# Row-tiled leftovers of the down projection in one block, on an S5 + SwiGLU layer

## The chip, the cores and the metric

One core of a Trainium2 chip. The metric is the device time of one execution in microseconds; each kernel is run several times and the median is shown. The profile is of one execution, of which it has every instruction of the engines: TensorE (PE; its weight loads apart as PEld), VectorE (DVE), ScalarE (ACT), GpSimd (POOL) and the queue of SyncE (SP), which here issues nearly all DMAs.

## The reference

A layer norm, and beside each other a diagonal state space model and a SwiGLU feed-forward, added to the input. 2048 tokens, width 512, 512 complex states, hidden width F = 1376.

```python
xn = layernorm(x)                                   # over 512, no weights
# A: state space model
Lam_bar = exp(exp(log_dt) * Lam)
Bu = xn @ B_bar.T                                   # complex, B_bar = ((Lam_bar - 1) / Lam) * B
h[t] = Lam_bar * h[t-1] + Bu[t]                     # 2048 steps
yA = 2 * real(h @ C.T) + xn * Dskip
# B: feed-forward
yB = (silu(xn @ w_gate) * (xn @ w_up)) @ w_down
out = x + yA + yB
```

1376 is 10 x 128 + 96: ten whole tiles of the hidden width, and 96 rows left over. These leftovers are what the change is about.

## The kernel before

The tokens go through in four chunks of 512 (`CH`), each of four tiles of 128. For each chunk:

- layer norm of four tiles into `xn_sb` (`ln_chunk`; statistics on DVE, rstd on POOL; chunks 2 and 3 are normalised on ACT, `ln_apply_act`, L503), then one DMA transpose into `xnT` (`xt_chunk_dma`; chunk 2's transpose lands in a part of the scratch tile `scrC`);
- gate and up matmuls with the hidden width on the partitions (`ffn_gate`, `ffn_up`, L716), 2 x 4 matmuls of 512 columns into a pair of PSUM banks; ACT makes `sg` = silu of the one (L728) and copies the other to `uf` (L785), DVE multiplies them into `hT` (L787);
- B matmuls (L836), copied by ACT to `u_sb` (L843); on DVE a rotation (L867), the scan (L876) and the rotation back into `hss`;
- down and C matmuls (`dc_chunk`), which sum into one bank for each tile of 128 tokens: a "down pass" of ten matmuls with `hT` for each of the four tiles (L919), and then, tile after tile, one leftover matmul of 96 rows (L933, `hL` by the last 96 rows of `w_down`) and eight C matmuls (L936); DVE adds the bank to `x_sb` (L941), in which input and skip stand by then (`resid_chunk`), and SP stores the tile.

The gate and up leftovers of all four chunks are done in one go after chunk 1's matmuls (`ffn_left`, L798 and L808; L808 uses half the columns of the array for each of two chunks), and DVE leaves their products in `hL`, 96 rows for each chunk.

In the last chunk the last tile is done in two pieces, 416 and 96 columns, so that the final addition and store are small.

Order of the work. Every instruction group is a task of a graph (`g.add`, `dma`) with its reads and writes. TensorE and SP keep the order of the program text; for ACT, DVE and POOL a list scheduler (`_schedule`) picks the next task by estimated times and the longest path behind it. `od` holds order edges that carry no data. `_plan` then works out which semaphores a task has to wait for, and `_emit` writes one `wait_ge` after the other ahead of the instruction. The eight PSUM banks are handed out in pairs by `next_pair`. The text order of the last part is: gate and up of chunk 3, `resid_chunk(2)`, `resid_chunk(3)`, `dc_chunk(2)`, `dc_chunk(3, split_last=True)`.

Of the kernel before, what the change touches and what calls it, by code (L numbers as in the profile page):

```python
# [10 lines left out]
ALU = alu_op_type.AluOpType  # L11
F32 = mybir.dt.float32
B16 = mybir.dt.bfloat16
# [171 lines left out]
def _plan(tasks, streams, new_sem, eng_sems):  # L185
    consumers = defaultdict(list)
    for t in tasks:
        for d in t.deps:
            consumers[d].append(t)
    for t in tasks:  # L190
        if t.dma:
            t.nsig = True
        else:
            t.nsig = any((c.eng != t.eng) or (t.eng != "pe") or c.dma for c in consumers[t])
    for eng, st in streams.items():
        lvl = 0
        for t in st:
            if t.dma:
                t.sem = new_sem("dma%d" % t.idx)
                t.lvl = 16  # L200
            elif t.nsig:
                lvl += 1
                t.sem = eng_sems[eng]
                t.lvl = lvl
    pos = {e: 0 for e in streams}
    known = {e: {} for e in streams}
    done = set()
    remaining = sum(len(s) for s in streams.values())
    while remaining:
        progressed = False  # L210
        for eng, st in streams.items():
            while pos[eng] < len(st):
                t = st[pos[eng]]
                if any(d not in done for d in t.deps):
                    break
                kn = known[eng]
                waits = {}
                for d in t.deps:
                    if d.eng == eng and eng == "pe" and not d.dma and not t.dma:
                        continue  # L220
                    k = id(d.sem)
                    if kn.get(k, 0) >= d.lvl:
                        continue
                    if k not in waits or waits[k][1] < d.lvl:
                        waits[k] = (d.sem, d.lvl)
                for d in t.deps:
                    for k, v in d.vc.items():
                        if kn.get(k, 0) < v:
                            kn[k] = v
                t.waits = list(waits.values())  # L230
                t.vc = dict(kn)
                if t.sem is not None:
                    t.vc[id(t.sem)] = max(t.vc.get(id(t.sem), 0), t.lvl)
                done.add(t)
                pos[eng] += 1
                remaining -= 1
                progressed = True
        assert progressed, "deadlock in static schedule"
# [11 lines left out]
def bass_parallel_sum__ssm_conv_s5__swiglu_ffn__prompt_kernel(  # L250
# [17 lines left out]
    Fh = B_w_gate.shape[1]  # L268
# [6 lines left out]
    PT = P // 128  # L275
    FT = (Fh + 127) // 128
    fsz = [min(128, Fh - i * 128) for i in range(FT)]
# [3 lines left out]
    g = _Graph()  # L281
    es = ExitStack()
    with es:
# [33 lines left out]
        tt1 = scrC[:, 1024:2048].rearrange("p (b t) -> p b t", b=2)  # L317
        tz = scrC[:, 2048:3072].rearrange("p (b t) -> p b t", b=2)
        xnT2 = scrC[:, 2048:3072].bitcast(B16).rearrange("p (j k t) -> p j k t", j=4, k=KT)
        xnT = [xnT01[:, 0], xnT01[:, 1], xnT2, xnT3]  # L320
        wtmp = scrC[:, 0:2048].rearrange("p (k d) -> p k d", k=4)
        NUS = 8
# [47 lines left out]
        def next_pair():  # L370
            for _ in range(NB // 2):
                b = 2 * (pair_ctr[0] % (NB // 2))
                pair_ctr[0] += 1
                if not (b in reserved or _bank_live(b) or _bank_live(b + 1)):
                    return b
            raise AssertionError("all PSUM pairs live")
# [4 lines left out]
        def BK(b):  # L381
            return [("bk", b, 0), ("bk", b, 1)]
# [407 lines left out]
        def ffn_left():  # L790
# [22 lines left out]
            for c, bk in zip((0, 2), pairs):  # L813
                sl = gctr[0] % NG
                gctr[0] += 1
                ul = uctr_f[0] % NUF
                uctr_f[0] += 1
                g.add("act", lambda e, sl=sl, bk=bk: e.activation(out=sg[0:NG0, sl].rearrange("p a t -> p (a t)"), in_=pair_f32(slice(0, NG0), bk), func=AF.Silu),
                      reads=BK(bk) + BK(bk + 1), writes=[("sg", sl)], name="silul%d" % c, est=917)
                g.add("act", lambda e, ul=ul, bk=bk: e.activation(out=uf[NU0:NG0, ul].rearrange("p a t -> p (a t)"), in_=pair_f32(slice(NG0, 128), bk), func=AF.Identity),  # L820
                      reads=BK(bk) + BK(bk + 1), writes=[("uf", ul)], name="uevx%d" % c, est=917)
                for k in range(2):
                    g.add("act", lambda e, k=k, ul=ul, c=c: e.activation(out=uf[0:NU0, ul, k, :], in_=pbank[64 * k:64 * k + NU0, bu + c // 2, :], func=AF.Identity),  # L823
                          reads=BK(bu + c // 2), writes=[("uf", ul)], name="uevl%d_%d" % (c, k), est=490)
                g.add("dve", lambda e, sl=sl, ul=ul, c=c: e.tensor_tensor(out=hL[0:NG0, c:c + 2, :], in0=sg[0:NG0, sl], in1=uf[0:NG0, ul], op=ALU.mult),
                      reads=[("sg", sl), ("uf", ul)], writes=[("hL", c + k) for k in range(2)], name="hmull%d" % c, est=611)

        usctr = [0]
        uctr = [0]
# [69 lines left out]
                    g.add("dve", lambda e, t1_=t1_, t3_=t3_, q_=q_: e.tensor_tensor(out=car[:, c + 1, 0, q_], in0=t3_, in1=t1_, op=ALU.subtract), reads=[("sm", "ct3", ph), ("sm", "ct1", ph)], writes=[("car", c + 1, ph)], name="c5_%d_%d" % (c, ph), est=70)  # L899
                    g.add("dve", lambda e, t2_=t2_, t4_=t4_, q_=q_: e.tensor_tensor(out=car[:, c + 1, 1, q_], in0=t4_, in1=t2_, op=ALU.add), reads=[("sm", "ct4", ph), ("sm", "ct2", ph)], writes=[("car", c + 1, ph)], name="c6_%d_%d" % (c, ph), est=70)  # L900

        def dc_chunk(c, split_last=False):
            hb = c % 2
            n = FT + 2 * PT
            items = []
            for lt in range(4):
                if split_last and lt == 3:
                    items.append((lt, 0, 416))
                    items.append((lt, 416, 96))
                else:  # L910
                    items.append((lt, 0, 512))
            prs = [next_pair() for _ in range((len(items) + 1) // 2)]
            banks = [prs[k // 2] + k % 2 for k in range(len(items))]

            def add_A(lt, c0, nc_, bk):
                def mmA(e, bk=bk, lt=lt, hb=hb, c=c, c0=c0, nc_=nc_):
                    for i in range(FL):
                        fs = fsz[i]
                        inst = e.matmul(pbank[:, bk, 0:nc_], lhsT=hT[0:fs, hb, i, lt * 128:(lt + 1) * 128], rhs=wd[0:fs, i, c0:c0 + nc_], start=(i == 0), stop=False)  # L919
                    return inst  # L920
                g.add("pe", mmA, reads=[("hT", hb, i) for i in range(FL)] + [("wd", 0)],
                      writes=BK(bk), name="mm_dA%d_%d" % (4 * c + lt, c0), est=FL * (216 if nc_ == 512 else nc_ * 0.43), ninst=FL)
            for it, bk in zip(items, banks):
                if it[2] >= 256:
                    add_A(*it, bk)
            for (lt, c0, nc_), bk in zip(items, banks):
                a = 4 * c + lt
                if nc_ < 256:
                    add_A(lt, c0, nc_, bk)

                def mmB(e, bk=bk, lt=lt, hb=hb, c=c, c0=c0, nc_=nc_):
                    j = FT
                    e.matmul(pbank[:, bk, 0:nc_], lhsT=hL[0:NG0, c, lt * 128:(lt + 1) * 128], rhs=wd[0:NG0, FL, c0:c0 + nc_], start=False, stop=False)  # L933
                    for pt in range(PT):
                        for ri in range(2):
                            inst = e.matmul(pbank[:, bk, 0:nc_], lhsT=hss[:, hb, pt, ri, lt * 128:(lt + 1) * 128], rhs=W12[:, ri, pt, c0:c0 + nc_], start=False, stop=(j == n - 1))  # L936
                            j += 1
                    return inst
                g.add("pe", mmB, reads=[("hL", c), ("wd", 1)] + [("hss", hb, pt) for pt in range(PT)] + [("W", ri, pt) for ri in range(2) for pt in range(PT)],
                      writes=BK(bk), name="mm_dB%d_%d" % (a, c0), est=(2 * PT + 1) * (216 if nc_ == 512 else nc_ * 0.43), ninst=2 * PT + 1)  # L940
                g.add("dve", lambda e, bk=bk, a=a, c0=c0, nc_=nc_: e.tensor_tensor(out=x_sb[:, a, c0:c0 + nc_], in0=pbank[:, bk, 0:nc_], in1=x_sb[:, a, c0:c0 + nc_], op=ALU.add),  # L941
                      reads=BK(bk) + [("x", a)], writes=[("xo", a, c0)], name="oadd%d_%d" % (a, c0), est=(660 if nc_ == 512 else 100 + nc_))
                dma("st_out%d_%d" % (a, c0), out_v[:, a, c0:c0 + nc_], x_sb[:, a, c0:c0 + nc_], writes=[("out", a, c0)], nbytes=TILEB * nc_ // 512,
                    reads=[("xo", a, c0)], out_=True)

        ffn_gate_quarters([0, 1, 2, 3])
        params_a()
# [40 lines left out]
            ffn_up(3, ip)  # L988
        resid_chunk(2)
        resid_chunk(3)  # L990
        dc_chunk(2)
        dc_chunk(3, split_last=True)

        _DBG["smi"] = dict(SMI)
        _DBG["sbuf_left"] = nc.sbuf_bytes_remaining
# [42 lines left out]
```

## Time and profile before

| | |
|---|---|
| timed runs, us | 178.19, 178.90, 179.28; median 178.9 |
| the profiled execution | 178.13 us, span of the instructions 176.3 us |
| busy, us | PE 173.0, DVE 161.8, ACT 86.1, PEld 82.4, POOL 11.3 |
| chain that ended last | PE 96% of the span |
| TensorE clock granted | full, throughout |
| matmuls L919 / L936 / L933 | 170 / 136 / 17 |
| DMA | 12.37 MB, 70 GB/s over the span |

Busy times of TensorE overlap from one matmul to the next (a 512-column matmul is shown with 379 ns, but they start 216 ns apart), so starts are compared and not lengths. The chain is followed backwards from the last instruction. Releasers of a wait are inferred. POOL's times are rough.

### The profile page before, as it was taken

Reading aid. Unit: us, or ns where it says so; the run is one execution under the profiler, and the core shown is the slowest. Engines: PE = TensorE matmul, PEld = TensorE weight load, DVE = VectorE, ACT = ScalarE, POOL = GpSimd, SP = SyncE. Lnnn points to the kernel's source line nnn. Section 1 sums busy time; section 2 is a strip of 40 time slices with the busy share of each in tenths; the row PEclk is TensorE's granted clock in tenths of the full one; section 3 lists DMA queues with packets and bytes.
Section 4 is the critical chain, followed back from the end, with each engine's and each line's share of the span. In section 5 each row is a group of like instructions: output and inputs, shape, how many; then the busy total and the mean of one; then the engine's idle time right before and its main releaser. Section 6 shows DMA issues by size and latency. Waiting matters only on the chain.

```text
span 176.3 us, 2356 instructions
## 1 busy us (share of the span) xinstructions
PE 173.0 (98%) x914; PEld 82.4 (47%) x914; DVE 161.8 (92%) x277; ACT 86.1 (49%) x113; POOL 11.3 (6%) x22
## 2 busy tenths in 40 slices
PE   7899999999999999999999999999999999999995
PEld 2794444444444444444444444444444444444443
DVE  2873999999999999999999999999999999999953
ACT  4479989899999579220456564000265620000000
POOL 3040500344000000000000000000000000000000
PEclk9999999999999999999999999999999999999999
DMA  5897565566559000002100000001100000000132
GB/s 173 272 368 187 119 114 179 162 132 131 149 205 123 0 0 0 0 4 86 35 0 0 0 0 4 0 0 59 59 0 4 0 0 0 0 0 4 42 118 78
DMA packets 22967, 12.37 MB, mean 70 GB/s; under 512 B 15309, under 2 KB 22957, under 8 KB 22957
## 3 DMA queue, kind: packets, MB, share of 16 engines
q1 hardware_dynamic: 22652, 11.77, 25.0%
q10 hardware_dynamic: 304, 0.46, 0.8%
q8 instruction: 7, 0.11, 0.3%
q14 instruction: 4, 0.02, 0.0%
HBM read 6.46 MB, written 2.10 MB: 49 GB/s over the span
## 4 chain that ended last, share of the span: by engine, by line
PE 96%; DMA 1%; DVE 1%; ACT 0%; issue 0%
PE pb L716 36%; PE pb L919 20%; PE pb L936 16%; PE pb L836 16%; PE pb L759 4%; PE pb L933 2%; PE pb L798 2%; DMA x_sb<-in_A_x_dram 1%; PE pb L808 1%; PE pb L543 1%; DVE st L512 0%; DVE xn_sb L495 0%; ACT xnT L554 0%; DVE x_sb L941 0%; ACT sd L514 0%
## 5 line engine op out<-in xcount | busy, mean ns | idle before, releaser
L876 DVE TENSOR_TENSOR_SCAN rot<-sm,car,rot 128x512 bf16<-128x512 f32 x32 | 38.7, 1265 | 0.0
L728 ACT ACTIVATE sg<-pb 128x1024 bf16<-128x1024 f32 x20 | 20.1, 1023 | 33.0 <-PE pb L716 31.9
L919 PE MATMUL pb<-wd,hT 128*128 128x512 bf16 (+2 forms) x170 | 35.4, 367 | 0.0
L936 PE MATMUL pb<-W,hss 128*128 128x512 bf16 (+2 forms) x136 | 30.4, 366 | 0.0
L716 PE MATMUL pb<-xnT,wu 128*128 128x512 bf16 x120 | 27.9, 379 | 0.0
L919 PEld LDWEIGHTS pb<-wd,hT 128*128 128x128 bf16 x170 | 16.1, 98 | 18.9 <-ACT uf L823 0.4
L785 ACT ACTIVATE uf<-pb 128x1024 bf16<-128x1024 f32 x20 | 20.5, 1025 | 7.9 <-PE pb L716 7.4
L716 PE MATMUL pb<-xnT,wg 128*128 128x512 bf16 x92 | 21.8, 379 | 0.0
L836 PE MATMUL pb<-xnT,BT 128*128 128x512 bf16 x96 | 21.0, 379 | 0.0
L936 PEld LDWEIGHTS pb<-W,hss 128*128 128x128 bf16 x136 | 12.8, 97 | 14.9
L843 ACT ACTIVATE u_sb<-pb 128x1024 bf16<-128x1024 f32 x16 | 16.1, 1020 | 5.6 <-PE pb L836 5.5
L716 PEld LDWEIGHTS pb<-xnT,wu 128*128 128x128 bf16 x120 | 11.7, 98 | 14.2 <-issue 0.2
L836 PEld LDWEIGHTS pb<-xnT,BT 128*128 128x128 bf16 x96 | 9.4, 98 | 11.3
L941 DVE TENSOR_TENSOR x_sb<-pb,x_sb 128x512 bf16<-128x512 f32 (+2 forms) x17 | 10.9, 655 | 3.8 <-PE pb L936 3.2
L787 DVE TENSOR_TENSOR hT<-sg,uf 128x1024 bf16<-128x1024 bf16 x20 | 13.5, 681 | 0.7 <-ACT uf L785 0.7
L716 PEld LDWEIGHTS pb<-xnT,wg 128*128 128x128 bf16 x92 | 9.0, 98 | 10.6
L479 DVE BATCH_NORM_STATS2 st<-x_sb 128x6 f32<-128x512 bf16 x12 | 7.5, 678 | 3.0 <-DMA x_sb<-in_A_x_dram 3.0
L867 DVE TENSOR_TENSOR rot<-u_sb,cosT 128x2048 bf16<-128x2048 bf16 x8 | 9.7, 1217 | 0.0
L867 DVE TENSOR_TENSOR rot<-rot,sin 128x2048 bf16<-128x2048 bf16 x8 | 9.8, 1219 | 0.0
L867 DVE TENSOR_TENSOR rot<-u_sb,sin 128x2048 bf16<-128x2048 bf16 x8 | 9.7, 1215 | 0.0
L867 DVE TENSOR_TENSOR rot<-rot,cosT 128x2048 bf16<-128x2048 bf16 x8 | 9.7, 1212 | 0.0
L867 DVE TENSOR_TENSOR rot<-rot 128x2048 bf16<-128x2048 bf16 x8 | 9.6, 1216 | 0.0
(87 smaller groups left out, 175.8 us busy)
## 6 DMA issues: line engine op xcount, KB each, us to landing
out_dram<-x_sb SPq DMA_DIRECT2D x15, 128.0 KB, 1.7
x_sb<-in_A_x_dram SPq DMA_DIRECT2D x3, 512.0 KB, 4.4
wd<-in_B_w_down_dram SPq DMA_DIRECT2D x1, 1280.0 KB, 6.3
wu<-in_B_w_up_dram SPq DMA_DIRECT2D x1, 768.0 KB, 4.9
wu<-in_B_w_up_dram SPq DMA_DIRECT2D x1, 608.0 KB, 7.1
x_sb<-in_A_x_dram SPq DMA_DIRECT2D x4, 128.0 KB, 3.5
wg<-in_B_w_gate_dram SPq DMA_DIRECT2D x1, 480.0 KB, 5.9
wg<-in_B_w_gate_dram ACTq DMA_DIRECT2D x1, 448.0 KB, 3.8
```

The costliest lines, as they stand in the source:

```text
L479: return g.add("dve", lambda e, a=a: e.bn_stats(out=st[:, a % 8, :], in_=x_sb[:, a, :]), reads=[("x", a)], writes=[("st", a % 8)], name="b ...
L716: inst = e.matmul(pbank[0:fs, bk, :].rearrange("p (j t) -> p j t", j=4), lhsT=w[:, kt, i * 128:i * 128 + fs], rhs=xnT[c][:, :, kt, :], sta ...
L728: g.add("act", lambda e: e.activation(out=sg[rows, sl, 0:n, :].rearrange("p a t -> p (a t)"), in_=pair_f32(rows, bk, 512 * n), func=AF.Sil ...
L785: g.add("act", lambda e: e.activation(out=uf[rows, ul, 0:n, :].rearrange("p a t -> p (a t)"), in_=pair_f32(rows, bk, 512 * n), func=AF.Ide ...
L787: g.add("dve", lambda e: e.tensor_tensor(out=hT[rows, hb, i0:i0 + n, :], in0=sg[rows, sl, 0:n, :], in1=uf[rows, ul, 0:n, :], op=ALU.mult), ...
L836: inst = e.matmul(pbank[:, bk, :].rearrange("p (j t) -> p j t", j=4), lhsT=BT[:, ri, kt, pt * 128:(pt + 1) * 128], rhs=xnT[c][:, :, kt, :] ...
L843: g.add("act", lambda e: e.activation(out=u_sb[:, us].rearrange("p r t -> p (r t)"), in_=pair_f32(slice(0, 128), b0), func=AF.Identity), r ...
L867: tt = lambda out, a, b, op, r, w, nm: g.add("dve", lambda e: e.tensor_tensor(out=out, in0=a, in1=b, op=op), reads=r, writes=w, name="%s_% ...
L876: g.add("dve", lambda e, A0=A0, A1=A1, k=k, ri=ri, pt=pt: e.tensor_tensor_scan(out=A1[:, k, ri, :], data0=rr[:, pt:pt + 1].to_broadcast([1 ...
L919: inst = e.matmul(pbank[:, bk, 0:nc_], lhsT=hT[0:fs, hb, i, lt * 128:(lt + 1) * 128], rhs=wd[0:fs, i, c0:c0 + nc_], start=(i == 0), stop=F ...
L936: inst = e.matmul(pbank[:, bk, 0:nc_], lhsT=hss[:, hb, pt, ri, lt * 128:(lt + 1) * 128], rhs=W12[:, ri, pt, c0:c0 + nc_], start=False, sto ...
L941: g.add("dve", lambda e, bk=bk, a=a, c0=c0, nc_=nc_: e.tensor_tensor(out=x_sb[:, a, c0:c0 + nc_], in0=pbank[:, bk, 0:nc_], in1=x_sb[:, a, ...
```

## The change

It has three parts.

1. `dc_chunk(2)` and `dc_chunk(3, split_last=True)` become `dc_last(2)`. The down passes of chunks 2 and 3 stand one after the other, in all eight banks. Then one block, `mmL`, does the leftovers of both chunks (all but the last 96 columns): the 96 rows are cut into three slices of 32, and each of the four token tiles `lt` has its operands on the partitions 32 `lt` to 32 `lt` + 31, so that 24 matmuls of 32 rows take the place of eight of 96. Then follow the C passes of both chunks, and the last piece of 96 columns as before. The operands are copies made by twelve new DMAs on SP: `wdL` (the leftover rows of `w_down`, four times) and `hR` (pieces of `hL`, eight), in parts of `scrC` that are free once W is prepared. All matmuls of the block have the tile size 32 x 128.
2. Chunk 2's normalisations on ACT get order edges: tile 9 after the copy of the third B unit of chunk 1, tile 10 after the fourth, tile 11 after the silu of chunk 1's first gate pair. In the program as built, tile 8 comes after the third copy, 9 after the fourth, and 10 and 11 after that silu; the cosine of the last state tile moves from ahead of them to behind them.
3. A task's waits are emitted in the order in which the planner expects them to end (DMAs first), the last one next to the instruction.

```diff
-                for d in t.deps:
+                for d in sorted(t.deps, key=lambda d: (not d.dma, d.fin, d.idx)):
...
                     if k not in waits or waits[k][1] < d.lvl:
+                        waits.pop(k, None)
                         waits[k] = (d.sem, d.lvl)
...
+        NL = 3
+        wdL = scrC[:, 0:768].bitcast(B16).rearrange("p (s d) -> p s d", s=NL)
+        hR = scrC[:, 768:1152].bitcast(B16).rearrange("p (c s t) -> p c s t", c=2, s=NL)
...
+            for r in range(4):
+                dma("ld_wdL%d" % r, wdL[32 * r:32 * r + 32, :, :], B_w_down[FL * 128:Fh, :].rearrange("(i s) d -> i s d", s=NL), [("wdL", r)], NG0 * 1024, after=tuple(alias_H))
+            for c in (2, 3):
+                for r in range(4):
+                    dma("hR%d_%d" % (c, r), hR[32 * r:32 * r + 32, c - 2, :, :], hL[0:NG0, c, r * 128:(r + 1) * 128], [("hR", c, r)], NG0 * 256, reads=[("hL", c)], after=tuple(alias_H))
...
+        def dc_last(c0):
+            items = []
+            for c in (c0, c0 + 1):
+                for lt, bk in enumerate(dc_banks()):
+                    w = 416 if (c, lt) == (c0 + 1, 3) else 512
+                    items.append((c, lt, w, bk))
+                    dc_A(c, lt, 0, w, bk)
+
+            def mmL(e):
+                for h in (items[:4], items[4:]):
+                    for k in range(NL):
+                        for c, lt, w, bk in h:
+                            inst = e.matmul(pbank[:, bk, 0:w], lhsT=hR[32 * lt:32 * lt + 32, c - 2, k, :], rhs=wdL[32 * lt:32 * lt + 32, k, 0:w], start=False, stop=False)
+                return inst
+            g.add("pe", mmL, reads=[("hR", c, r) for c in (2, 3) for r in range(4)] + [("wdL", r) for r in range(4)],
+                  writes=sum([BK(it[3]) for it in items], []), name="mm_dL", est=2 * NL * 216 + 200, ninst=2 * NL * 4)
+            for c, lt, w, bk in items:
+                dc_B(c, lt, 0, w, bk, 0)
+            bk = next_pair()
+            dc_A(c0 + 1, 3, 416, 96, bk)
+            dc_B(c0 + 1, 3, 416, 96, bk, 1)
...
-        dc_chunk(2)
-        dc_chunk(3, split_last=True)
+        dc_last(2)
+
+        by_name = {t.name: t for t in g.tasks}
+        for nm, prev in (("xn9", "uev_b1_2"), ("xn10", "uev_b1_3"), ("xn11", "silu1_0")):
+            by_name[nm].od.add(by_name[prev])
```

`dc_A` is the down pass of one tile, `dc_B` its C pass (with the leftover matmul where its last argument is 1), addition and store; both are the code of `dc_chunk` cut in two. Chunks 0 and 1 keep their leftover matmul of 96 rows.

More of the change, by code (lines that the diff above doesn't have):

```diff
@@ L900, in ssm_elem_chunk, with dc_A @@
                     g.add("dve", lambda e, t2_=t2_, t4_=t4_, q_=q_: e.tensor_tensor(out=car[:, c + 1, 1, q_], in0=t4_, in1=t2_, op=ALU.add), reads=[("sm", "ct4", ph), ("sm", "ct2", ph)], writes=[("car", c + 1, ph)], name="c6_%d_%d" % (c, ph), est=70)
-        def dc_chunk(c, split_last=False):
+        def dc_A(c, lt, c0, nc_, bk):
             hb = c % 2
-            n = FT + 2 * PT
-            items = []
[L906 to L944, printed above, removed]
@@ new lines, in mmA, with dc_B, mmB @@
+            def mmA(e):
+                for i in range(FL):
+                    inst = e.matmul(pbank[:, bk, 0:nc_], lhsT=hT[:, hb, i, lt * 128:(lt + 1) * 128], rhs=wd[:, i, c0:c0 + nc_], start=(i == 0), stop=False)
+                return inst
+            g.add("pe", mmA, reads=[("hT", hb, i) for i in range(FL)] + [("wd", 0)],
+                  writes=BK(bk), name="mm_dA%d_%d" % (4 * c + lt, c0), est=FL * (216 if nc_ == 512 else nc_ * 0.43), ninst=FL)
+        def dc_B(c, lt, c0, nc_, bk, left):
+            hb = c % 2
+            a = 4 * c + lt
+            def mmB(e):
+                if left:
+                    e.matmul(pbank[:, bk, 0:nc_], lhsT=hL[0:NG0, c, lt * 128:(lt + 1) * 128], rhs=wd[0:NG0, FL, c0:c0 + nc_], start=False, stop=False)
+                for pt in range(PT):
+                    for ri in range(2):
+                        inst = e.matmul(pbank[:, bk, 0:nc_], lhsT=hss[:, hb, pt, ri, lt * 128:(lt + 1) * 128], rhs=W12[:, ri, pt, c0:c0 + nc_], start=False, stop=(pt == PT - 1 and ri == 1))
+                return inst
+            g.add("pe", mmB, reads=([("hL", c), ("wd", 1)] if left else []) + [("hss", hb, pt) for pt in range(PT)] + [("W", ri, pt) for ri in range(2) for pt in range(PT)],
+                  writes=BK(bk), name="mm_dB%d_%d" % (a, c0), est=(2 * PT + left) * (216 if nc_ == 512 else nc_ * 0.43), ninst=2 * PT + left)
+            g.add("dve", lambda e: e.tensor_tensor(out=x_sb[:, a, c0:c0 + nc_], in0=pbank[:, bk, 0:nc_], in1=x_sb[:, a, c0:c0 + nc_], op=ALU.add),
+                  reads=BK(bk) + [("x", a)], writes=[("xo", a, c0)], name="oadd%d_%d" % (a, c0), est=(660 if nc_ == 512 else 100 + nc_))
+            dma("st_out%d_%d" % (a, c0), out_v[:, a, c0:c0 + nc_], x_sb[:, a, c0:c0 + nc_], writes=[("out", a, c0)], nbytes=TILEB * nc_ // 512,
+                reads=[("xo", a, c0)], out_=True)
@@ new lines, in dc_banks, with dc_chunk @@
+        def dc_banks():
+            prs = [next_pair() for _ in range(2)]
+            return [prs[lt // 2] + lt % 2 for lt in range(4)]
+        def dc_chunk(c):
+            banks = dc_banks()
+            for lt in range(4):
+                dc_A(c, lt, 0, 512, banks[lt])
+            for lt in range(4):
+                dc_B(c, lt, 0, 512, banks[lt], 1)
+        def dc_last(c0):
+            items = []
+            for c in (c0, c0 + 1):
[8 more added lines that the diff above has]
+                            inst = e.matmul(pbank[:, bk, 0:w], lhsT=hR[32 * lt:32 * lt + 32, c - 2, k, :], rhs=wdL[32 * lt:32 * lt + 32, k, 0:w], start=False, stop=False)
+                return inst
+            g.add("pe", mmL, reads=[("hR", c, r) for c in (2, 3) for r in range(4)] + [("wdL", r) for r in range(4)],
[5 more added lines that the diff above has]
+            dc_B(c0 + 1, 3, 416, 96, bk, 1)
```

## The prediction

> **What bounds the kernel now.** I read the page first, for the busy time of each engine with its share of the span, and for the shares of the chain that ended last.
>
> ```profile
> PE 173.0 (98%) x914; PEld 82.4 (47%) x914; DVE 161.8 (92%) x277; ACT 86.1 (49%) x113; POOL 11.3 (6%) x22
> ...
> PE 96%; DMA 1%; DVE 1%; ACT 0%; issue 0%
> ```
>
> A busy PE alone proves little, since matmul ends are modelled. So I read the chain in order of time next (start, length in us, line, number of instructions): do its stretches come out at a constant rate per matmul, or is there waiting hidden in them?
>
> ```profile
> 10.49 2.23 PE pb L759 x40
> ...
> 65.39 1.85 PE pb L808 x16
> 67.23 8.74 PE pb L919 x40
> ...
> 141.62 8.63 PE pb L919 x40
> 150.25 0.22 PE pb L933
> 150.47 1.73 PE pb L936 x8
> ...
> 158.04 8.23 PE pb L919 x40
> ...
> 172.11 0.18 PE pb L933
> 172.29 1.41 PE pb L936 x8
> 173.70 0.42 PE pb L919 x10
> ...
> 174.55 0.26 DVE x_sb L941
> ```
>
> The down pass of chunk 2 is 40 matmuls in 8.63 us: 0.2158 us each. Eight C matmuls take 1.73 (0.216 each), one 96-row leftover (L933) 0.22, as much as a full 128-row one. From 12.7 us to 174.5 us every stretch keeps this rate, apart from two places of 0.1 us around L808. TensorE is the bound, with no stall to take away, so an edit pays only by what it saves in matmul time, and costs only what puts a gap between matmuls.
>
> **The change, part by part.**
>
> *Leftovers removed.* Chunks 2 and 3 lose eight L933 matmuls: four and three of 512 columns, one of 416. 7 x 0.2158 + 0.18 = 1.69 us off the bounding engine. The 96-column piece keeps its own (0.04).
>
> *The row-tiled block added.* 24 matmuls of 32 rows in six rounds of four; the four of a round sit in different row groups, go to different banks, and may run together. No 32-row matmul is in this trace. The nearest rows are the column-tiled pairs of L808, in the view of TensorE's instructions in order of time (start, length):
>
> ```profile
> 64.36 1.03 PE L798 MATMUL pb<-xnT,wg 128*128 128x512 bf16 x4
> 65.32 1.05 PE L808 MATMUL pb<-xnT,wu 128*64 128x512 bf16 x8
> ...
> 66.85 0.38 PE L808 MATMUL pb<-xnT,wu 128*64 128x512 bf16 x1
> 67.17 1.04 PE L919 MATMUL pb<-wd,hT 128*128 128x512 bf16 x4
> ```
>
> Sixteen half-width matmuls start as eight pairs 0.216 us apart: the two of a pair do run together. At the edges there is a price. Four L798 matmuls starting at 64.36 make room at 64.36 + 4 x 0.2158 = 65.22, but the first pair starts at 65.32; the last pair starts at 66.85, room is at 67.07, and the next full matmul starts at 67.17. So 0.10 us in, 0.10 us out. For the new block, lower bound: 6 x 0.2158 = 1.29, plus 0.20 for the edges, 1.49. Upper bound, tiles one after the other: 24 x 0.2158 + 0.20 = 5.38. Between them two others: weights, four loads a round, at the rate of the L759 stretch where each 128-column matmul has its own load (2.23 / 40 = 0.056 us), need 4 x 0.056 = 0.223 a round, 1.34 in all; and rounds that do not overlap at all, with the full 0.379 us length of a matmul plus 0.10 of a weight load, 6 x 0.48 + 0.20 = 3.07. I take 0.22 a round, so 1.32 + 0.20 = 1.52, because L808 is the only tiled work on this chip that the trace holds and it keeps the 0.216 us beat with its loads a beat ahead. Net of the two: 1.52 - 1.69 = -0.17 us; bounds -0.20 and +3.69.
>
> The Trainium skill, "TensorE: Matmul & The Clock Gate", Part 3 (Measured speedup vs the span model), speaks against the change: packing four K=32, N=512 row tiles measured 3.07 times, not 4. By it a round would be an estimated 4 x 0.216 / 3.07 = 0.28 us, the block 1.69 + 0.20 = 1.89, and the net +0.2 us, a small loss. The row of L808 shows a beat without that loss, though with two tiles and not four; no run yet shows four.
>
> *Twelve waits ahead of the block.* It waits for twelve DMAs, long since landed. Queued behind are all of the C matmuls of chunks 2 and 3, and behind them the additions, the stores and the end. Handling one satisfied wait is bounded by the "issue" pieces of the chain, 0.02 to 0.05 us, so the eleven extra are 0.2 to 0.6 us if exposed, and nothing if TensorE's queue has them done while the 40 matmuls of chunk 3's down pass (8.23 us) run. I take nothing: the trace has waits before most groups of matmuls and no gap at them. Upper bound +0.6.
>
> *The twelve DMAs themselves* stand on SP's queue between chunk 3's transpose and the first store. The weight pieces wait for the last W preparation (DVE, 72.6 us) and the hL pieces for the second hL product (76.9 us). At about 0.5 us of issue each (0.43 to 0.71 in SP's rows) SP is busy until about 81, so the first store goes from 78.7 to 81 and SP has caught up two stores later, since stores come 1.95 us apart. Nobody waits for these stores. The block needs the data at 158.5, so some 70 us hide them; without that cover they would cost their 6 us of issue plus a landing (1.7 us for a 128 KB store).
>
> *Chunk 3's down pass moves ahead of chunk 2's C pass*, from 158.04 to 150.25. It needs chunk 3's last product and its banks.
>
> ```profile
> 142.81 0.68 DVE L787 TENSOR_TENSOR hT<-sg,uf 128x1024 bf16<-128x1024 bf16 x1
> ...
> 159.40 2.35 DVE L867 TENSOR_TENSOR hss<-rot 128x2048 bf16<-128x2048 bf16 x2
> ...
> 165.20 1.28 DVE L941 TENSOR_TENSOR x_sb<-pb,x_sb 128x512 bf16<-128x512 f32 x2
> ```
>
> In DVE's order of time the product is done at 143.5, 6.7 us early, and ACT's last copy out of a bank ends at 142.7. Chunk 3's C pass would start at 158.5 + 1.5 + 6.9 = 166.9, and its hss is there at 161.75. Chunk 2's additions (L941) do not run before 165.2 even now, because DVE is behind the state update and the residuals, so C results that come from 161.7 on delay no one; the fifth bank pair, for the 96-column piece, is free at 166.5 and wanted at 173. Cost 0; cover 5 us or more each.
>
> *Chunk 2's normalisation on ACT.*
>
> ```profile
> 36.49 2.91 ACT L503 ACTIVATE xn_sb<-x_sb,nmr,rstd 128x512 bf16<-128x512 bf16 x4
> 39.31 1.91 ACT L843 ACTIVATE u_sb<-pb 128x1024 bf16<-128x1024 f32 x2
> ```
>
> Today the four normalisations hold up two copies (39.31 to 41.2); TensorE takes the first copy's banks at 41.05 with room from about 40.3, 0.8 us to spare. In the new order I walk ACT with these lengths (copy 0.92, normalisation 0.8, sine 0.62): the two copies end near 37.2 and 38.9, the last normalisation near 42.2 instead of 39.4, the last cosine near 42.9 instead of 36.5, the next copy (L785) ends 0.8 us later. Three things come late. On SP, the transpose of chunk 2 goes from 41.14 to about 42.2, and behind it the w_down loads and chunk 3's transpose by the same 1.1; they land near 46.6, 52.8 and 58, wanted at 54.9, 67.2 and 63.5. On DVE, the product L787 and the second half of chunk 0's rotation come up to 0.8 us late, of which the 0.34 us that DVE idles at 52.4 takes some back; the first C pass needs W (72.6) and hL (73.2) at 75.8, 2.6 us of cover. POOL's rstd stays ahead of it. All hidden: 0 in the profiled run. A larger slip than the cover would cost TensorE the difference.
>
> *Ordered waits.* They place the wait that ends last next to the instruction. On the chain only the first transpose has two waits (its "issue" piece is 0.05 where others have 0.02): -0.03 at best, 0 at worst.
>
> **Sum.** -1.69 + 1.52 - 0.03 = -0.2 us on the profiled execution: 178.13 (span 176.3) becomes 177.9. That execution is 0.8 us below the median of the three timed runs and at their fast end, so I subtract the same from the median: 178.9 - 0.2 = 178.7 us, no change within 1% (1.8 us is about what a measurement of this kernel can tell from no change).
>
> **Rivals.**
>
> *The four row tiles do not run together (slower).* Place: the block at 158.5. For it: nothing in the trace has four tiles or 32 rows, and four weight sets have to be loaded in the time of one matmul. Against: the pairs of L808. Break-even is (1.69 - 0.20) / 6 = 0.25 us a round; over 1% slower from (1.69 + 1.79 - 0.20) / 6 = 0.55 us a round. Fully serial it is +3.7: 182.6 us.
>
> *Rounds overlap partly*, because loads of a row group wait for its matmul: up to 0.48 a round, +1.4, with the exposed waits +2.0; middle 179.9 us, mostly within 1%. For it: four loads in 0.216 us leave no slack against 0.223. Against: the loads of L808 run a beat ahead.
>
> *The ACT order matters more than the profile shows.* The timed runs spread over 1.1 us, and the 0.8 us to spare at 41.05 is the thinnest in the middle of the kernel; if slower executions stall there, the new order saves up to 0.8: 178.0 us. Against: the profiled run shows no stall at all, and the spread may come from the first load.
>
> *The block does nothing of note* (tile order or rate cancels the saving): 178.9; not to be told from my forecast.
>
> **How the numbers follow.** Forecast, with the nothing-of-note case, 0.67 (own range 178.0 to 179.3, the spread of the runs about it); ACT case 0.14; partly overlapped 0.10; serial 0.09. Over 1% faster needs 177.1, which only the ACT case with luck in the runs reaches: 0.05. Over 1% slower needs 180.7: the serial case and a quarter of the partly overlapped one, 0.12 with rounding up. Same: 0.83. The range for 8 in 10 runs from the ACT case less half of the runs' spread (178.0 - 0.5), 177.5, to the partly overlapped one, 180.0.
>
> **What would show it.** Right: TensorE's last 24 us with down passes back to back from 141.6, 24 matmuls labelled 32*128 starting in fours about 0.22 us apart, 0.1 us gaps on either side, C passes of eight without a leftover, the last matmul about 0.2 us earlier, and no new wait of TensorE. Wrong: 32-row matmuls starting one by one 0.2 us apart, a gap before the block (waits), a wait of TensorE on DVE near 75.8 or on a DMA near 55, or a C pass of chunk 3 waiting for hss.

## The result, and the profile after

| | before | changed |
|---|---|---|
| median of 22 runs, us | 178.56 | 178.07 |
| fastest and slowest of them, us | 178.19, 179.37 | 177.93, 178.66 |
| profiled execution, us (span) | 178.13 (176.3) | 178.49 (176.7) |

The ratio is 0.9971, 95% interval 0.9958 to 0.9984: 0.5 us faster, beyond the noise and within 1%. The fastest run gained 0.26 us and the slowest 0.71. The three runs of the kernel before that were shown ahead of the prediction had a median 0.3 us above that of these 22. One later run of the kernel before, 182.02 us at a granted clock of 0.991, is left out of the count at the end of the experiments.

The page and the chain of the changed kernel (start, length in us, line, number; L916 is the down pass, L962 the new block, L930 the C pass, L934 the addition; the chain goes through 21 of the block's 24 matmuls):

```profile
PE 173.2 (98%) x930; PEld 82.1 (46%) x930; DVE 162.1 (92%) x277; ACT 86.0 (49%) x113; POOL 11.1 (6%) x22
...
PE 96%; DMA 3%; ACTq 0%; DVE 0%; issue 0%
```

```profile
13.31 11.22 PE pb L720 x52
...
142.21 16.87 PE pb L916 x80
159.07 1.40 PE pb L962 x21
160.48 13.60 PE pb L930 x64
174.08 0.43 PE pb L916 x10
...
174.93 0.26 DVE x_sb L934
```

The profiled execution of the changed kernel is the longer one of the two, and the chain tells why that is no sign against the change. From chunk 2's first down matmul to the last addition it takes 174.93 - 142.21 = 32.72 us; before, 174.55 - 141.62 = 32.93. That is -0.21 us. From the first full-rate gate matmul to that point it is 142.21 - 13.31 = 128.90; before, 141.62 - 12.72 = 128.90, the same to the hundredth. The 0.59 us it is behind are all ahead of 13.31: TensorE waited for the first gate weights in this execution. These are all the waits of TensorE (who for whom, total, times, longest; L763 is the first gate matmuls, L478 the warm-up, L547 the first transposes, PEq TensorE's own sequencer):

```profile
PE pb L478 <- PEq L1052: 0.8, 1, 0.8
PE pb L763 <- DMA wg<-in_B_w_gate_dram: 0.6, 1, 0.6
PE pb L547 <- DVE xn_sb L499: 0.3, 1, 0.3
```

TensorE's last part in order of time, where starts can be compared:

```profile
142.04 17.03 PE L916 MATMUL pb<-wd,hT 128*128 128x512 bf16 x80
159.01 1.47 PE L962 MATMUL pb<-scrC 32*128 32x512 bf16 x24
160.41 13.67 PE L930 MATMUL pb<-W,hss 128*128 128x512 bf16 x64
```

The 80 down matmuls (70 of 0.2158 us, ten narrower ones of 0.176) leave room at 142.04 + 16.87 = 158.91; the block starts at 159.01 and the C pass at 160.41. So the block costs 0.10 to get in, 6 x 0.216 = 1.30 of beat, 0.10 to get out: 1.50 us for the 1.69 that went. The last part is very steady: in all six profiled executions with this block (five of them of experiments below) it takes 32.72 or 32.73 us, and in all four of kernels that keep the old leftover matmuls (three of them below) 32.93.

It is the start that moves. In the changed kernel without the ordered waits (an experiment below, profiled at 177.91 us) the first full-rate gate matmuls stand in the chain as

```profile
12.74 11.22 PE pb L719 x52
```

That is 0.57 us ahead of 13.31, and that execution is 0.58 us shorter than the profiled one of the changed kernel. So the first loads make a part of the spread of the timed runs.

ACT around chunk 1's B copies (L852) and the first normalisation (L507), where before four normalisations stood ahead of copies at 39.31:

```profile
36.93 1.01 ACT L852 ACTIVATE u_sb<-pb 128x1024 bf16<-128x1024 f32 x1
37.84 0.81 ACT L507 ACTIVATE xn_sb<-x_sb,nmr,rstd 128x512 bf16<-128x512 bf16 x1
38.54 1.02 ACT L852 ACTIVATE u_sb<-pb 128x1024 bf16<-128x1024 f32 x1
```

The third of the four B copies of chunk 1 ends at 37.9, 2.4 us earlier than before, although this execution started 0.6 us later. The remaining 0.3 us of the median's 0.5 had to be sought here or in the ordered waits.

### The profile page after: what moved, and what is told of

It is laid out like the page before. It is cut to its first block, busy times and chain, and to the rows that moved or that the text cites. A ratio compares the mean times of both kernels' runs of the same rounds, so it can differ in the third digit from the quotient of the medians.

```text
span 176.7 us, 2405 instructions
## 1 busy us (share of the span) xinstructions
PE 173.2 (98%) x930; PEld 82.1 (46%) x930; DVE 162.1 (92%) x277; ACT 86.0 (49%) x113; POOL 11.1 (6%) x22
## 4 chain that ended last, share of the span: by engine, by line
PE 96%; DMA 3%; ACTq 0%; DVE 0%; issue 0%
PE pb L720 36%; PE pb L916 20%; PE pb L930 16%; PE pb L845 16%; PE pb L763 4%; DMA wg<-in_B_w_gate_dram 3%; PE pb L802 2%; PE pb L812 1%; PE pb L927 1%; PE pb L962 1%; PE pb L547 0%; ACTq L405 0%; DVE x_sb L934 0%
## 5 line engine op out<-in xcount | busy, mean ns | idle before, releaser
L916 PE MATMUL pb<-wd,hT 128*128 128x512 bf16 (+2 forms) x170 | 35.2, 367 | 0.0
L930 PE MATMUL pb<-W,hss 128*128 128x512 bf16 (+2 forms) x136 | 29.3, 366 | 0.0
L916 PEld LDWEIGHTS pb<-wd,hT 128*128 128x128 bf16 x170 | 16.1, 98 | 18.9 <-ACT sg L822 0.4
L930 PEld LDWEIGHTS pb<-W,hss 128*128 128x128 bf16 x136 | 12.8, 97 | 15.1 <-issue 0.4
L852 ACT ACTIVATE u_sb<-pb 128x1024 bf16<-128x1024 f32 x16 | 16.3, 1020 | 5.3 <-PE pb L845 5.0
L934 DVE TENSOR_TENSOR x_sb<-pb,x_sb 128x512 bf16<-128x512 f32 (+2 forms) x17 | 10.9, 655 | 3.6 <-PE pb L930 2.9
```

Source lines behind the costliest of these rows:

```text
L852: g.add("act", lambda e: e.activation(out=u_sb[:, us].rearrange("p r t -> p (r t)"), in_=pair_f32(slice(0, 128), b0), func=AF.Identity), r ...
L916: inst = e.matmul(pbank[:, bk, 0:nc_], lhsT=hT[:, hb, i, lt * 128:(lt + 1) * 128], rhs=wd[:, i, c0:c0 + nc_], start=(i == 0), stop=False)
L934: g.add("dve", lambda e: e.tensor_tensor(out=x_sb[:, a, c0:c0 + nc_], in0=pbank[:, bk, 0:nc_], in1=x_sb[:, a, c0:c0 + nc_], op=ALU.add), r ...
```

## The experiments

Theories. T1: a fixed 0.2 us of matmul time in every execution is all there is. T2: that, and the new order of the normalisations takes a wait of TensorE out of those executions in which chunk 2's tokens land late. T3: the block and its order of passes narrow the spread. T4: the ordered waits do. T5: the spread comes from the first loads alone.

**Each part alone.** The changed kernel without parts 2 and 3; the kernel before with part 2 alone; the kernel before with part 3 alone.

```diff
 # block alone: the changed kernel without
-                for d in sorted(t.deps, key=lambda d: (not d.dma, d.fin, d.idx)):
+                for d in t.deps:
-                        waits.pop(k, None)
-        for nm, prev in (("xn9", "uev_b1_2"), ("xn10", "uev_b1_3"), ("xn11", "silu1_0")):
-            by_name[nm].od.add(by_name[prev])
 # normalisation alone: the kernel before with these last two lines
 # waits alone: the kernel before with the sorted() and the pop
```

> The block with its DMAs and the new order of passes, without the order edges for chunk 2's normalisation and without the ordered waits. Theory T1 (all of the gain is matmul time, 0.2 us): fastest and median both about 0.2 us below the kernel before, and the spread of the timed runs stays at about 1.2 us (178.0 to 179.2, median near 178.3). Theory T2 (the block gives 0.2 us to every execution, and the rest of the median's 0.5 us comes from chunk 2's normalisation, which takes a stall out of slower executions): the same here, -0.2 in fastest and median, spread unchanged. Rival T3 (the block and the new order of passes also narrow the spread): spread about 0.7 us and the median 0.5 below. In the profile: the block 1.40 us from its first matmul to the next C matmul, as in the changed kernel.

> Only the three order edges for chunk 2's normalisation. T1: nothing, 178.56 as before with the spread unchanged. T2: the fastest runs stay at 178.2, since no stall is to be taken from these; the slower ones (178.6 to 179.4) go away, the spread falls to about 0.7 us and the median to 178.25, 0.3 us below. T3: nothing. In the profile: the third B copy of chunk 1 ends near 37.5 and not at 40.3, ahead of TensorE's demand at 41 by 3 us.

> Only the ordered waits. T1 and T2: 0.0 to 0.05 us, not to be told from nothing; the spread stays. Rival T4 (the waits in planner's order are what makes slower executions fewer, because an engine that sits on the wrong semaphore first comes late to the others): the median 0.2 to 0.3 us below and the spread smaller.

| part alone | fastest | median | ratio to before (95%) |
|---|---|---|---|
| before, 35 runs beside them | 178.14 | 178.51 | |
| block | 177.94 | 178.26 | 0.9982 (0.9958 to 1.0006) |
| normalisation | 178.16 | 178.29 | 0.9982 (0.9963 to 1.0001) |
| ordered waits | 178.31 | 178.48 | 1.0019 (0.9985 to 1.0052) |

Taken alone none of the three is told from 1 by its interval, but the pattern is that of T2: the block moves the fastest run by 0.2 and leaves the spread (177.94 to 179.41); the normalisation leaves the fastest run and cuts the spread (178.16 to 178.89); the waits do neither. The two medians, -0.25 and -0.22, nearly add up to the -0.49 of the whole change. With twelve runs each this is a pattern and not yet a proof.

The profile of the block alone happened to be of one of its longer executions, 179.23 us. Its tail, 175.66 - 142.94 = 32.72, is that of the changed kernel. Most of its extra time is one gap of TensorE (in order of time; L719 is gate and up here, L482 the token statistics, L680 a cosine of the state tiles, L678 what DVE prepares for it, L506 the normalisation, L851 the B copy; idle time and what ended it in brackets):

```profile
39.60 1.89 PE L719 MATMUL pb<-xnT,wu 128*128 128x512 bf16 x8
42.36 1.90 PE L719 MATMUL pb<-xnT,wg 128*128 128x512 bf16 x8 [0.87 <-ACT u_sb L851]
```

```profile
23.72 1.76 SPq L399 DMA_TRANSPOSE xnT<-xn_sb  x1
29.62 0.93 SPq L404 DMA_DIRECT2D x_sb<-in_A_x_dram  x2
```

```profile
33.17 2.47 DVE L482 BATCH_NORM_STATS2 st<-x_sb 128x6 f32<-128x512 bf16 x4 [1.41 <-DMA x_sb<-in_A_x_dram]
```

```profile
37.20 1.34 ACT L680 ACTIVATE cosT<-scrC,halfpi 128x512 bf16<-128x512 f32 x2 [1.56 <-DVE scrC L678]
38.47 2.93 ACT L506 ACTIVATE xn_sb<-x_sb,nmr,rstd 128x512 bf16<-128x512 bf16 x4
41.31 1.91 ACT L851 ACTIVATE u_sb<-pb 128x1024 bf16<-128x1024 f32 x2
```

Read from the top: TensorE is done with one pair of banks at 39.60 + 8 x 0.2158 = 41.33 and starts on the next at 42.36, a loss of 1.03 us. SP issues the load of chunk 2's tokens at 29.62, behind chunk 1's transpose; in the profiled execution before it did so at 27.54 (its transpose began at 22.86 and landed sooner), so the lateness is handed down from earlier loads. DVE sits 1.41 us on these tokens and starts their statistics at 33.17, where the profiled execution before had them at 31.01 without a wait. What DVE prepares for two cosines stands behind the statistics, so ACT waits 1.56 us for it; the normalisations behind the cosines begin at 38.47 (before 36.49), the copy behind them starts at 41.31, and TensorE stands still for its banks.

**Late tokens on purpose.** One longer DMA brings the tokens of chunks 2 and 3 together, so that the statistics of chunk 2 wait for both; the engines keep their order. Same edit in both kernels.

```diff
-            dma("ld_x8", x_sb[:, 8:12, :], x_v[:, 8:12, :], ...)
-            dma("ld_x12", x_sb[:, 12:16, :], x_v[:, 12:16, :], ...)
+            dma("ld_x8", x_sb[:, 8:16, :], x_v[:, 8:16, :], ...)
+            dma("ld_x12", tch[0:16, 0:1], wg_v[0:128:8, 0:1, 0:2], ...)    # 64 bytes, to keep the order
```

> The kernel before, with chunk 2's tokens made late: one DMA of 1 MB brings the tokens of chunks 2 and 3, so chunk 2's statistics wait for both; every engine keeps its order. The tokens land about 1.5 us later (near 32.4 and not 30.9). Theory T2 (slower executions come from late loads, and the four normalisations hold the copy out of the banks that TensorE wants at 41): every execution now has a wait of TensorE on ACT's copy of about 0.6 us, the fastest near 178.8 and the median near 179.0, 0.4 to 0.7 above the kernel before. Rival T5 (the spread is made by the first loads alone and the middle of the kernel has cover): no change, 178.5.

> The same late tokens in the changed kernel. T2: no wait of TensorE, because the copies of chunk 1's B units stand ahead of the normalisations that wait for the tokens; median 178.1 as the changed kernel's, 0.9 below the kernel before with late tokens. T5: 178.1 too. If the changed kernel has only moved the thin place to another: a wait near 46 (gate copies) or 55 (chunk 2's transpose), and the time rises by 0.3 or more.

The kernel before: median 179.32, fastest 178.94, each 0.8 us above the 178.53 and 178.18 of the same kernel without the delay (somewhat more than the 0.4 to 0.7 expected; the ratio, 1.0032, 1.0012 to 1.0053, comes to 0.6). The changed kernel: 178.06, as without the delay (ratio 0.9977 to the kernel before without the delay, 0.9964 to 0.9990). Nearly the same lateness (DVE waits 1.69 us for the tokens in the one and 1.81 in the other) costs the one 0.8 us and the other nothing. The gap in the delayed kernel before, TensorE and then ACT in order of time:

```profile
42.28 1.90 PE L716 MATMUL pb<-xnT,wg 128*128 128x512 bf16 x8 [0.97 <-ACT u_sb L843]
```

```profile
37.12 1.34 ACT L677 ACTIVATE cosT<-scrC,halfpi 128x512 bf16<-128x512 f32 x2 [1.66 <-DVE scrC L675]
38.39 2.93 ACT L503 ACTIVATE xn_sb<-x_sb,nmr,rstd 128x512 bf16<-128x512 bf16 x4
41.23 1.91 ACT L843 ACTIVATE u_sb<-pb 128x1024 bf16<-128x1024 f32 x2
```

ACT of the delayed changed kernel (the third copy is the one at 38.11):

```profile
36.05 0.63 ACT L673 ACTIVATE sin<-scrC 128x512 bf16<-128x512 f32 x1 [1.70 <-DVE scrC L671]
36.59 1.01 ACT L852 ACTIVATE u_sb<-pb 128x1024 bf16<-128x1024 f32 x1
37.50 0.71 ACT L681 ACTIVATE cosT<-scrC,halfpi 128x512 bf16<-128x512 f32 x1
38.11 1.01 ACT L852 ACTIVATE u_sb<-pb 128x1024 bf16<-128x1024 f32 x1
39.01 0.81 ACT L507 ACTIVATE xn_sb<-x_sb,nmr,rstd 128x512 bf16<-128x512 bf16 x1
```

In the changed kernel too ACT waits 1.70 us for work of DVE that stands behind the late statistics. But the third copy ends at 39.12, and TensorE takes its banks at 41.67 without a wait, 2.5 us later: what is late (normalisations, transpose) now stands behind what is urgent. The edges moved a cosine and DVE's preparations with the normalisations; which of these moves does how much was not separated. T5 is out: the first loads do not make the spread alone. How much of the spread of the timed runs is made in this way stays an inference, since only one execution of a kernel is profiled; the wait is shown once as it happened and once forced.

**The order within the block.** Three matmuls of one row group after each other, then the next group.

```diff
-                    for k in range(NL):
-                        for c, lt, w, bk in h:
+                    for c, lt, w, bk in h:
+                        for k in range(NL):
```

> The changed kernel with the 24 row-tiled matmuls in another order: three of one row group after each other, then the next group. If matmuls of one row group wait for each other, start in order, and only neighbours of different groups run together, each half of the block takes 9 beats of 0.216 us (3 + 2 x 3) where it takes 3 now: 18 beats, 3.9 us, and the kernel is 2.6 us slower than the changed one, 180.7. If all 24 ran one by one in either order, there would be no difference (the changed kernel's 1.40 us already speaks against it). If the array can hold back a group and go on with the next, no difference either.

178.16 us, ratio 0.9965 (0.9944 to 0.9985): no difference. My main expectation, 2.6 us more, was wrong, and the last alternative in the text was right. TensorE's instructions from 158.9 to 159.1 us, and those from 160.1 to 160.3:

```profile
158.95 0.41 PE L962 MATMUL pb<-scrC 32*128 32x512 bf16 x4
```

```profile
159.81 0.62 PE L962 MATMUL pb<-scrC 32*128 32x416 bf16 x8
```

Four matmuls start within 0.03 us (0.41 less the 0.38 of one), though in the program the second and third belong to the row group of the first; a queue in order would have started them 0.216 and 0.43 us later. The second row shows it by the shape: the one that starts first there is 416 columns wide, the second of the three of that width and the 23rd of the 24 in the program; the seven listed with it start later, and only one of them comes after it in the program. Within a group the matmuls go one after the other (the next experiment), and the groups pass each other.

**Fewer row groups.** The four token tiles on two row groups.

```diff
 # in the operands of e.matmul; hR gets twice the room, and its copies go to the same two groups
-hR[32 * lt:32 * lt + 32, c - 2, k, :]
+hR[32 * (lt % 2):32 * (lt % 2) + 32, c - 2, lt // 2, k, :]
-wdL[32 * lt:32 * lt + 32, k, 0:w]
+wdL[32 * (lt % 2):32 * (lt % 2) + 32, k, 0:w]
```

> The changed kernel with the four token tiles on two row groups and not four (tiles 0 and 2 on partitions 0 to 31, tiles 1 and 3 on 32 to 63). If a row group works through its matmuls one by one and groups run beside each other, a group has 12 of them: 12 x 0.216 + 0.2 = 2.8 us for the block, 1.3 above the changed kernel's 1.5, and the kernel comes to 179.4. If the beat of 0.216 us were shared by whatever is in flight (all 24 in four lanes whichever rows they have), 178.1; if tiles did not run together at all, 24 beats, 5.4 us, 182.

179.41 us, 1.3 above the changed kernel, as expected. Its chain:

```profile
158.70 2.69 PE pb L962 x23
161.39 13.60 PE pb L930 x64
```

2.69 us for the block up to the next C matmul (1.40 with four groups): 12 x 0.2158 + 0.10, where four groups have 6 x 0.2158 + 0.10. The time is the number of matmuls of the fullest row group times the beat, and the edge.

**Two blocks in place of one**, one for each chunk, with chunk 2's C passes between.

```diff
-            def mmL(e):
-                for h in (items[:4], items[4:]):
+            for h in (items[:4], items[4:]):
+                def mmL(e, h=h):
...
-            for c, lt, w, bk in items:
-                dc_B(c, lt, 0, w, bk, 0)
+                for c, lt, w, bk in h:
+                    dc_B(c, lt, 0, w, bk, 0)
```

> The changed kernel with the block cut in two, one for each chunk: down passes of chunks 2 and 3, 12 tiled matmuls of chunk 2, its C passes, 12 tiled matmuls of chunk 3, its C passes. Theory T1 (a change of tile mode costs 0.1 us at each edge, and the rest of the block is the 0.216 us beat): two more edges, 0.2 us slower than the changed kernel, 178.27, so that the matmul part of the gain is used up; each block 3 x 0.216 + 0.09 us from its first matmul to the next C matmul, and 0.10 before it. Rival (the edges are a price for the whole block, such as its twelve waits): only one place with a gap before it, 178.1.

Median 178.33, fastest 178.20: 0.26 above the changed kernel's first runs, where 0.2 was expected; in its profile the last part takes 32.94 us, 0.22 above the changed kernel's. TensorE in order of time:

```profile
158.67 0.82 PE L962 MATMUL pb<-scrC 32*128 32x512 bf16 x12
159.43 7.08 PE L930 MATMUL pb<-W,hss 128*128 128x512 bf16 x31
166.44 0.82 PE L962 MATMUL pb<-scrC 32*128 32x512 bf16 x12
167.19 6.76 PE L930 MATMUL pb<-W,hss 128*128 128x512 bf16 x31
```

Each block holds the array 0.75 us (3 x 0.216 + 0.10), and the 32 C matmuls from 159.43 (one record is missing) leave room at 166.34 while the second block starts at 166.44: 0.10 in and 0.10 out, paid once more. The edge is a price of each change of tile size, not of the waits.

**The block without tiles.** Everything of the changed kernel, copies and waits included, but eight matmuls of 96 rows in the block.

```diff
-                for h in (items[:4], items[4:]):
-                    for k in range(NL):
-                        for c, lt, w, bk in h:
-                            inst = e.matmul(pbank[:, bk, 0:w], lhsT=hR[32 * lt:32 * lt + 32, c - 2, k, :], rhs=wdL[32 * lt:32 * lt + 32, k, 0:w], ...)
+                for c, lt, w, bk in items:
+                    inst = e.matmul(pbank[:, bk, 0:w], lhsT=hL[0:NG0, c, lt * 128:(lt + 1) * 128], rhs=wd[0:NG0, FL, 0:w], ...)
```

> The changed kernel with everything in place, the twelve DMAs and their waits too, but the block done with eight matmuls of 96 rows on the whole array. It tells the tiles from the new order of passes. Theory T1 (the matmul part of the gain is the tiles' alone): the block takes 1.69 us and no edges, 0.19 us more than the tiled one, 178.26. Rival (the order of the passes, or additions that come together, give a part): nearer to 178.07. No gap ahead of the block if twelve landed waits cost nothing; up to 0.6 if they do.

> The changed kernel once more, beside the untiled block on the same chip, since the untiled one's first timed runs stood on a chip where the kernel before was 0.3 us slower than elsewhere. T1: fastest and median 0.2 us below the untiled block's. Rival (the tiles give nothing, the order of passes all): equal.

> The untiled block again. T1: 0.2 us above the changed kernel of the same call in fastest and median, about 178.26 if the changed one is at 178.07. Rival: equal.

The first runs gave 178.45 (ratio 0.9962, 0.9929 to 0.9995) on a chip whose kernel before stood at 178.84, which could not be compared with the changed kernel's other runs. Side by side on one chip the changed kernel has 178.28 (fastest 178.05) and the untiled block 178.60 (fastest 178.28): 0.2 to 0.3 us apart. The kernel before had 178.51 there, so in this series the median of the changed kernel gains 0.23 us, about the block's part alone, and the untiled block, which has the new order of the normalisations too, gains nothing (ratio 1.0002, 0.9975 to 1.0030). The chain of the untiled block says what the tiles give without that noise:

```profile
142.25 16.87 PE pb L916 x80
159.12 1.69 PE pb L960 x8
160.81 13.50 PE pb L930 x64
...
175.15 0.26 DVE x_sb L934
```

175.15 - 142.25 = 32.90, against 32.72 of the changed kernel and 32.93 of the one before. The new order of the passes gives next to nothing (0.03); the tiles give 0.18. And the block begins where the down pass ends (70 x 0.2158 + 10 x 0.176 = 16.87): twelve landed waits ahead of it cost nothing.

**The changed kernel without the ordered waits.**

> The changed kernel with the waits in the old order. T1 and T2: the same as the changed kernel, 178.07, within 0.1. T4 (the ordered waits matter once the other two are there): 0.1 to 0.3 above.

178.12 us against 178.07, fastest 177.91 against 177.93: the ordered waits give nothing that can be measured, alone or with the rest. No version of these is faster than the changed kernel by more than the noise.

**All timed runs together.** Of 157 runs of kernels without the new order of the normalisations (the kernel before in its five series, the block alone, the waits alone; the delayed kernels are left out) 48 were more than 0.7 us above the fastest of their kernel and series; of 116 runs of the nine kernels with it, 9. This holds for the series of the untiled block too (7 of 23 before, one of 12 in each of the two kernels). So the new order does take away long executions, and the block alone (3 of 12) does not. A few of over 1.5 us remain with it (4 of 116); their cause was not found.

## Why the prediction was right, and where it was off

It said 178.7 us, range 177.5 to 180.0, no change within 1%; measured 178.07, in the range and within 1%, but the gain is 0.5 us where I had 0.2. Of the 0.63 us between the two, 0.34 are the median of only three runs that I started from, and 0.29 the gain. The range was wide enough for both; that it held says little about the second.

- *The block.* Right to a few hundredths, mechanism and size: 1.52 us predicted, 1.50 measured; removed 1.69; net -0.17 predicted, -0.21 in the chain (0.03 of it the new order of the passes). The rounds keep 0.216 us, as the pairs of L808 suggested, and each edge costs the 0.10 that I read from L808.
- *The rule that spoke against.* The Trainium skill, "TensorE: Matmul & The Clock Gate", Part 3 (Measured speedup vs the span model), with its 3.07 times, would have made a round 0.28 us and the net a loss of 0.2. Here 24 matmuls take six beats, the full four times between the edges, and the measurement decides.
- *The serial rival and the partly overlapped one.* Both wrong on four groups. That matmuls of one row group go one after the other was right in kind: with two groups the block takes 2.69 us.
- *Twelve waits, DMAs, the moved down pass.* Zero each, as predicted. (The bound for exposed waits, 0.02 to 0.05 us each, was read too low: the chain has an "issue" piece of 0.14 at 5.26. Nothing was exposed.) The copies of hL took SP 0.71 us each and not 0.5, so the first store left at 83.2 and not 81; nobody waited.
- *The normalisation on ACT: the step that was mis-sized.* In the profiled execution it is zero, as I had it. But I carried that zero over to the median with the words "so I subtract the same from the median". The profile was of an execution in which the tokens came in time; late tokens use up the 0.8 us of cover at 41.05, as the block alone showed in one execution (1.03 us lost) and the delayed kernel before even in its fastest run (0.8 us). I had this as a rival (0.14, up to 0.8 us; with the block's 0.2 its 178.0 should have been 177.9); it was not a rival but a second term beside the first. On the median it measured 0.2 to 0.3 us in the first runs (normalisation alone -0.22, whole change less block -0.24; the interval of the former just takes in no change) and nothing in the series of the untiled block; what holds in all series is that long executions become fewer. My other account of the spread, the first load, was right for a part of it (0.57 us between two executions).
- *Ordered waits.* -0.03 at best predicted; 178.12 without them, nothing to be seen.

## What to carry to other kernels

When one engine is gapless in a profile, look for the place where it is only just gapless: a cover of 0.8 us against loads that came 2 us later in one execution than in another is a cost in the longer runs that a single profile does not show, and delaying one load shows it at once. Put copies that free a bank for the bounding engine ahead of work that waits for a DMA. Row tiles pay by count: here 0.2 us for each excursion into another tile size, and one beat for each matmul of the fullest row group, so leftovers are worth collecting into one block, and cutting the block in two gave the gain away.

## What the runs showed of the hardware

- The row groups of the array do not keep one order among them. With three matmuls of a group issued in a row the first matmuls of the four groups still started within 0.03 us, and the block took 1.42 us (1.40 in the interleaved order). The Trainium skill, "TensorE: Matmul & The Clock Gate", Part 3 (The mechanism), has matmuls in strict program order in start and end; these starts are not: the 23rd of 24 in the program started at 159.81, ahead of six that stand before it.
- Row tiles of 32 rows keep the beat of full matmuls: 24 in 1.30 us of beat, with four weight loads in each 0.216 us (90 to 94 ns each in the records, overlapping).
- Eleven satisfied waits more in front of a TensorE instruction cost no time behind a down pass of 16.87 us: the untiled block starts where the pass ends.
